# A quarter of one weight pair loaded in other row groups, and other runs of unused matmuls near the end

## The chip, the cores and the metric

The kernel runs on one core of one Trainium2 chip. A core has a matmul engine (TensorE, PE in the profile, with its weight loads as PEld), three engines for elementwise work (VectorE or DVE, ScalarE or ACT, GpSimd or POOL) and SyncE (SP), which here only starts output transfers. Transfers between main memory and the on-chip memory are carried out by 16 DMA engines that all queues share; a transfer counts as landed when the parts of all 16 have arrived. The metric is the time of one execution on the device in microseconds (us). Lower is better.

## The reference

The first half is attention for 8 batches, 8 heads, 576 positions and head size 64. Half of the heads look back over 32 neighbouring positions, the other half over 32 positions that are 4 apart. The second half takes the attention output as 4608 tokens of 512 numbers and runs a soft mixture of 8 experts with 4 slots each:

```
attn = softmax(mask(q @ k.T / 8)) @ v            # per batch and head
x = attn as [4608, 512]
logits = x @ phi                                  # phi [512, 32]
d = softmax over the tokens; slot_input = d.T @ x # 32 slots of 512
for e in range(8):                                # w1 [8,512,1024], w2 [8,1024,512]
    slot_out[e] = relu(slot_input[e] @ w1[e]) @ w2[e]
out = softmax over the slots(logits) @ slot_out   # [4608, 512]
```

The weights w1 and w2 hold 16.8 MB each in float32. They are used only once the slots of all tokens are summed, and each of their numbers is used for four slots alone.

## The kernel before, in words

**Attention.** The work is cut into 8 units: a pair of batches times a kind of head. For each unit GpSimd starts six loads of q, k and v (L425), which turn float32 into bfloat16 on the way into one of three slots of the buffer `stg`. TensorE transposes the unit (L566 or L571) into the buffer `TT`, multiplies q with k (L609), ScalarE takes the exponential (L616), VectorE masks it (L624), TensorE multiplies with v (L663), VectorE divides (L674), and so on up to the logits (L718) and the slot sums (L766). All these tiles go through the 8 banks of the accumulator memory, two at a time.

**Who decides the order.** Operations are listed in Python with a cost, a key and their dependences, and a planner (`Prog.schedule`) simulates the engines and fixes one order per engine. Dependences become waits on semaphores, one for each engine and one for each load. Loads are all issued by GpSimd in the order of the list, outputs all by SyncE. Where the planner sees TensorE idle inside a fixed window, it places runs of matmuls whose result nobody reads (L987).

**Weights.** `wload` fetches the weights under the attention and beyond it. The w1 parts go to `WD` and to a free stretch of `stg`. The w2 experts come in pairs: p3a (a part of the fourth pair) and p0, p1, p2 (the first three pairs), p3b and p3c (the rest of the fourth pair). They lie in places that attention no longer needs: p3a, p0 and p1 in `stg` (L469 for most, L458 to L463 for p0), p2, p3b and p3c in `TT`. One engine takes its share of these loads strictly in the order in which GpSimd issues them: w17, p3a, p0, p1, p2, p3b, p3c.

**The pair p0 is loaded in a special way.** Each of 128 partitions (rows) gets two runs of 4096 numbers. Rows 0 to 95 come as two ordinary loads (L458), one for each run. The last 32 rows, a quarter, come as four loads of 8 rows (L463), with one tiny load of 8 rows of 2 x 32 numbers into an unused buffer `scr` (L461) between the third and the fourth. All seven share one semaphore, `s_p0`.

**After attention.** A short chain on TensorE, VectorE and ScalarE computes the first expert layer (L838), folds it (L858) and copies it to `hT` (L867). Then the second layer runs part by part (L885) as the parts of w2 have landed, in the order p3a, p0, p1, p2, p3b, p3c. Between them stand the sums for the softmax over slots (`rsum`, L912) and one run of 7 unused matmuls (`keep`, L901), which is placed after p2. The sum of all parts is scaled into `so_sb` by VectorE and ScalarE (L923 and L927), and the last stage multiplies it with the token weights (L955, L957). VectorE and ScalarE take turns in scaling the results into float32 (L970, L969), and SyncE sends them out in six transfers of growing size (L978), 9.44 MB in all.

Of the kernel before, what the change touches and what calls it, by code (L numbers as in the profile page):

```python
# [52 lines left out]
class Op:  # L53
    n = 0
# [75 lines left out]
class Prog:  # L130
# [7 lines left out]
    def op(self, e, fn, r=(), w=(), a=(), alloc=(), cost=0.5, key=0.0, mode="f",  # L138
           sem=None, nbytes=0, nd=0, nq=1, ni=2, after=()):
        o = Op(e, fn, cost, key, mode)  # L140
        deps = list(after)
        for b in r:
            deps += b.ready
        for b in w:
            b.fresh()
            deps += b.prev
        for b in a:
            deps += b.prev
        seen = set()
        for d in deps:  # L150
            if d.id not in seen:
                seen.add(d.id)
                o.deps.append(d)
        for b in r:
            b.reads.append(o)
        for b in list(w) + list(a):
            b.ready.append(o)
        o.wr = [b for b in list(w) + list(a) if b.pool is not None]
        for b in list(r) + list(w) + list(a):
            if b.pool is not None and b not in o.touch:  # L160
                b.left += 1
                o.touch.append(b)
        o.alloc = list(alloc)
        o.sems = sem
        o.ni = ni + 2
        o.dma = nbytes / 435e3 + 0.011 * nd / 16 + 0.022 * nq
        self.ops.append(o)
        return o
# [149 lines left out]
def bass_dilated_sliding_attn__then__soft_moe_slots_kernel(  # L318
# [12 lines left out]
    op = P.op  # L331

    def sb(name, shape, dt=BF16):
        return A(nc.sbuf_tensor(name, shape, dt))

    WARM = 7
    NPT, NVN, NXB, NXT, NET = 6, 5, 5, 4, 2
    WD = sb("WD", [128, 7, 4096])
    stg = sb("stg", [128, 3, 9216])
# [22 lines left out]
    h_sb = sb("h_sb", [128, FF])  # L362
    hT = sb("hT", [128, 16, 128])
    half = sb("half", [128, 2, 32])
    scr = sb("scr", [8, 2, 32])
    so_sb = sb("so_sb", [128, DM])

    ps = A(nc.psum_tensor("ps", [128, 8, 512], F32))
# [11 lines left out]
    def tile(pool, size=1):  # L380
        t = Buf(pool)
        t.size = size
        return t
# [4 lines left out]
    def pair(t):  # L388
        return ps[:, t.phys[0]:t.phys[0] + 2, :]

    def bank(t):
        return ps[:, t.phys[0], :]
# [10 lines left out]
    b_mask = [Buf(), Buf()]  # L403
    b_id0, b_id, b_sel, b_fold, b_rowm, b_phist, b_phi = [Buf() for _ in range(7)]
# [36 lines left out]
    def wload(name):  # L441
        ap, b = HOME[name]
        b.prev = [o for al in b.al for o in al.ready + al.reads]
        sem = DmaSem(nc, f"s_{name}")
        if name[:2] == "w1":
            src = moe_w1[int(name[2:])].rearrange("(p c) f -> p c f", c=4)
            dst = ap.rearrange("p (c f) -> p c f", c=4)
        else:
            g = int(name[1])
            c = {"": slice(0, 16), "a": slice(0, 8), "b": slice(8, 14), "c": slice(14, 16)}[name[2:]]  # L450
            src = moe_w2[2 * g:2 * g + 2].rearrange("e (p c) f -> (e p) c f", c=16)[:, c, :]
            dst = ap.rearrange("p (c f) -> p c f", f=512)
        if name == "p0":
            src = src.rearrange("p (x c) f -> p x (c f)", x=2)
            dst = ap.rearrange("p (x y) -> p x y", x=2)[:, :, 0:4096]

            def skewed(g):
                res = [g.dma_start(dst[0:96, x], src[0:96, x]) for x in range(2)]  # L458
                for r in (96, 99, 97, None, 98):
                    if r is None:  # L460
                        res.append(g.dma_start(scr[:], src[0:8, :, 0:32]))  # L461
                    else:
                        res.append(g.dma_start(dst[r:128:4], src[r:128:4]))  # L463
                return res
            op("pool", skewed, after=b.prev, a=[b], cost=4.2, sem=sem, nbytes=512 * 8192, nd=288,
               nq=7)
            return
        cut = [slice(None)]
        op("pool", lambda g: [g.dma_start(dst[:, x], src[:, x]) for x in cut], after=b.prev, a=[b],  # L469
           cost=0.6 * len(cut), sem=sem, nbytes=512 * ap.shape[1], nd=128 * len(cut), nq=len(cut))  # L470

    for e in range(7):
# [12 lines left out]
       w=[b_phist], cost=0.1, sem=s_phi, nbytes=65536)  # L485
# [5 lines left out]
       r=[b_id0], w=[b_id], cost=1.6)  # L491
# [4 lines left out]
    def asel(t, sl, base, pat, cm):  # L496
# [7 lines left out]
       r=[b_mask[0]], w=[b_mask[1]], cost=0.6)  # L504
# [11 lines left out]
    for i, t in enumerate(VNt):  # L516
# [6 lines left out]
       cost=0.1, key=1)  # L523
    op("dve", lambda g: g.memset(half[:], 0.0), w=[b_half], cost=0.1, key=1)
    for x in range(2):
        for j in range(4):
# [3 lines left out]
               r=[b_id], w=[b_half], cost=0.1, key=1)  # L530
    for j in range(4):
        op("dve", lambda g, j=j: g.tensor_copy(fold[32 * j:32 * j + 32, :],
                                               ident[32 * j:32 * j + 32, 32 * j:32 * j + 32]),
           r=[b_id], w=[b_fold], cost=0.1, key=1)
    for j in range(4):
        op("dve", lambda g, j=j: g.tensor_copy(phi_pad[:, :, j, :], phi_st[:]),
           r=[b_phist], **{"w" if j == 0 else "a": [b_phi]}, cost=0.2, key=1)
# [244 lines left out]
    for u in range(NU):  # L782
# [28 lines left out]
    K1 = 1000.0  # L811
    op("dve", lambda vv: vv.tensor_reduce(rcs[:], csum[:], mybir.AxisListType.X, AluOp.add),
       r=[b_csum], w=[b_rcs], cost=0.1, key=K1)
# [3 lines left out]
    def pe_f(t):  # L817
# [9 lines left out]
        r=[fo], w=[b_siT], cost=0.25, key=K1)  # L827
# [5 lines left out]
    for hh in range(2):  # L833
        def pe(t, hh=hh):
            for c in range(4):
                for hi in range(2):
                    for j in range(4):
                        i_ = t.matmul(pair(hp)[32 * j:32 * j + 32, hh, :], siT[:, 512 * hi + 128 * c + 32 * j:  # L838
                                                       512 * hi + 128 * c + 32 * j + 32],
                                      w1v[2 * j + hi][:, c, 512 * hh:512 * hh + 512],  # L840
                                      start=(c == 0 and hi == 0), stop=(c == 3 and hi == 1))
            return i_
        ffn1 = op("pe", pe, r=[b_siT] + w1b, a=[hp], w=[b_hp[hh]], alloc=[hp] if hh == 0 else [],
                  cost=1.8, mode="c", key=K1, ni=64)
        if hh == 0:
            op("act", lambda ac: ac.activation(h_sb[:, 0:512], pair(hp)[:, 0, :], ACTF.Relu),
               r=[b_hp[0], hp], w=[b_h[0]], cost=0.65, key=K1)
        else:
            op("dve", lambda vv: vv.tensor_scalar(h_sb[:, 512:1024], pair(hp)[:, 1, :], 0.0, None,
                                                  op0=AluOp.max),  # L850
               r=[b_hp[1], hp], w=[b_h[1]], cost=0.65, key=K1)
    for p_ in range(2):
        ht = tile(psum, 1)

        def pe(t, p_=p_, ht=ht):
            for c in range(8):
                for x in range(2):
# [4 lines left out]
                 key=K1, ni=32)  # L862
# [16 lines left out]
    for k_, (name, g, c0, c1) in enumerate(PARTS):  # L879
        wv = HOME[name][0].rearrange("p (c f) -> p c f", f=512)  # L880
        for h_ in range(2):
            def pe(t, k_=k_, name=name, g=g, c0=c0, c1=c1, h_=h_, wv=wv):
                for c in range(c0, c1):
                    j = c % 4
                    i_ = t.matmul(pair(sp_)[32 * j:32 * j + 32, h_, 0:256],  # L885
                                  hT[:, c, 24 * g:24 * g + 32],
                                  wv[:, c - c0 + (1 if name == "p0" and c > 7 else 0), 256 * h_:256 * h_ + 256],
                                  start=(k_ == 0 and c < c0 + 4), stop=(k_ > 3 and c >= 12))
                return i_
            last_ = op("pe", pe, r=b_hT + [HOME[name][1]], alloc=[sp_] if k_ == h_ == 0 else [],  # L890
                       a=[sp_, b_sp[h_]], cost=0.13 * (c1 - c0) / 4, mode="c",
                       ni=2 * (c1 - c0),
                       key=K1 + 2 + 0.5 * k_ + 0.1 * h_)
            if k_ == 2:
                mid = last_
        if k_ == 3:
            warm = tile(psum, 1)

            def keep(t, warm=warm):
                for _ in range(WARM):  # L900
                    i_ = t.matmul(bank(warm)[:, 0:512], ident[:, :],  # L901
                                  mask[0][:].rearrange("p m x -> p (m x)")[:, 0:512],
                                  start=True, stop=True)
                return i_
            op("pe", keep, r=[b_id, b_mask[0]], w=[warm], alloc=[warm], cost=0.216 * WARM,
               ni=2 * WARM, key=K1 + 3.9, after=[last_])
    rs = tile(psum, 1)

    def rsum(t):
# [6 lines left out]
       after=[mid])  # L916
    op("dve", lambda vv: vv.reciprocal(rtok[:], bank(rs)[:, 0:N_TOK // 128]), r=[rs], w=[b_rtok],
       cost=0.2, key=K1 + 1)

    for h_ in range(2):  # L920
        sl = slice(256 * h_, 256 * h_ + 256)
        if h_ == 0:
            op("dve", lambda vv, sl=sl: vv.tensor_scalar(so_sb[:, sl], pair(sp_)[:, 0, 0:256],  # L923
                                                         rcs[:, 0:1], None, op0=AluOp.mult),
               r=[b_sp[0], b_rcs], w=[b_so[0]], cost=0.35, key=K1 + 20)
        else:
            op("act", lambda ac, sl=sl: ac.activation(so_sb[:, sl], pair(sp_)[:, 1, 0:256],  # L927
                                                      ACTF.Copy, scale=rcs[:, 0:1]),
               r=[b_sp[1], b_rcs], w=[b_so[1]], cost=0.4, key=K1 + 20)
# [12 lines left out]
    for o, (t0, n) in enumerate(TILES):  # L942
# [4 lines left out]
        for j0 in range(0, n, 2):  # L947
# [4 lines left out]
            for j in range(2 if split else min(2, n - j0)):  # L952
                def pe(t, o=o, po=po, j0=j0, j=j, split=split):
                    if split:
# [5 lines left out]
                        w=[b_po[j]], alloc=[po] if j == 0 else [], after=[p0] if j else [],  # L960
                        cost=0.12 if split else 0.22, key=kk + 0.01 * j)
                col = rcol[o] + (0 if split else j0 + j)

                def ev(en, po=po, ost=ost, j=j, j0=j0, split=split, col=col):
# [3 lines left out]
                    if en is nc.scalar:  # L968
# [3 lines left out]
                        cost=0.35 if split else 0.6, key=kk)  # L972
# [7 lines left out]
            r=[ob], cost=0.1, sem=so, nbytes=262144 * n, key=K1 + 30 + o)  # L980
# [60 lines left out]
```

## Time and profile before

Four runs of the kernel gave 180.01, 180.35, 180.52 and 181.2 us, with a median of 180.44 us.

| what | value |
|---|---|
| time of the profiled execution | 180.01 us |
| its span, first to last instruction | 178.3 us |
| mean granted TensorE clock | 0.911 |
| TensorE busy (matmul) | 136.0 us, 76% |
| VectorE busy | 112.9 us, 63% |
| ScalarE busy | 96.2 us, 54% |
| GpSimd busy | 37.7 us, 21% |
| read from main memory | 61.93 MB |
| written to main memory | 9.44 MB |
| loads issued by GpSimd (software queue) | 84.1% of the 16 DMA engines' span |

How to read it: "busy" is the time in which an engine ran an instruction. The "slices" view cuts the span into 40 equal parts and prints the busy share of each in tenths. PEclk is the clock that the chip grants TensorE, in tenths of full speed. The DMA line is the mean busy share of the 16 DMA engines. The "chain" follows the last instruction back to what released it, step by step. A "window" gives the same sums for one stretch of time; its last three columns are the granted clock, the DMA share and the rate in GB/s of bytes written. All times in the views are counted from the start of the span.

The trace also has a record for every packet that a DMA engine moved (start, duration, bytes) and for every arrival of an engine's part of a load. The records don't name the engine.

### The profile page before, as it was taken

How to read it: one execution, taken by the hardware profiler on the slowest of the kernel's cores; microseconds unless marked ns; L12 is line 12 of the kernel's file. 1: busy time of each engine (PE TensorE's matmuls, PEld its weight loads, DVE VectorE, ACT ScalarE, POOL GpSimd, SP SyncE). 2: the span in 40 equal slices, each digit the busy share in tenths (PEclk: the TensorE clock that was granted, in tenths of full speed). 3: DMA queues.
4: the chain of work that ended last, by engine and by line, in shares of the span. 5: the costliest groups of instructions: out<-in, count | busy, mean ns of one | idle time of the engine just before them, and what ended most of it. 6: DMA issues, size and time to landing. Idle time of an engine off the chain costs nothing.

```text
span 178.3 us, 5788 instructions
## 1 busy us (share of the span) xinstructions
PE 136.0 (76%) x2609; PEld 104.7 (59%) x2609; DVE 112.9 (63%) x256; ACT 96.2 (54%) x141; POOL 37.7 (21%) x75
## 2 busy tenths in 40 slices
PE   0019799777999877999967899978999997798000
PEld 0019687666797676798856788855556684342000
DVE  6850588766677992998979587998250200699300
ACT  2005889474695962878956688783211000599000
POOL 7990707034003300800103400102000000000000
PEclk9999999995699996999999699997899999699755
DMA  5999999999999999999999999999999996299995
GB/s 81 196 213 213 217 215 209 218 217 214 211 217 214 219 208 212 215 219 214 220 208 215 213 219 213 215 219 204 230 210 210 223 194 123 91 409 461 450 471 235
DMA packets 6056, 40.80 MB, mean 229 GB/s; under 512 B 1808, under 2 KB 1808, under 8 KB 2448
## 3 DMA queue, kind: packets, MB, share of 16 engines
q0 software_dynamic: 4640, 30.94, 84.1%
q1 hardware_dynamic: 1392, 9.50, 12.8%
q8 instruction: 20, 0.33, 0.7%
q14 instruction: 4, 0.03, 0.0%
HBM read 61.93 MB, written 9.44 MB: 400 GB/s over the span
## 4 chain that ended last, share of the span: by engine, by line
PE 38%; DMA 22%; DVE 19%; issue 6%; ACT 5%; POOL 2%; DVEq 0%; POOLq 0%
DMA TT<-in_moe_w_dram 17%; PE ps L571 8%; PE ps L566 6%; DMA stg<-in_k_dram 5%; PE ps L609 4%; DVE WD L970 4%; PE ps L663 4%; DVE PT L624 4%; PE ps L634 4%; PE ps L718 4%; DVE XB L674 4%; DVE VN L639 3%; PE ps L691 3%; ACT TT L591 2%; ACT PT L616 2%
## 5 line engine op out<-in xcount | busy, mean ns | idle before, releaser
L616 ACT ACTIVATE PT<-ps 128x768 bf16<-128x768 f32 x48 | 37.1, 811 | 10.4 <-PE ps L609 10.0
L591 ACT ACTIVATE TT<-ps 128x864 f32<-128x864 f32 x32 | 28.5, 896 | 18.6 <-PE ps L571 15.8
L674 DVE TENSOR_TENSOR XB<-ps,RV 96x768 bf16<-96x768 f32 x32 | 30.4, 951 | 0.9
L571 PE MATMUL ps<-ident,stg 96*64 96x96 bf16 x576 | 17.5, 225 | 13.9 <-DMA stg<-in_k_dram 12.8
L639 DVE COPY VN<-ps 128x768 bf16<-128x768 bf16 x32 | 17.1, 542 | 12.0 <-PE ps L634 11.9
L571 PEld LDWEIGHTS ps<-ident,stg 96*64 96x64 bf16 x576 | 15.6, 124 | 15.2 <-DMA stg<-in_k_dram 12.8
L663 PE MATMUL ps<-VN,PT 128*128 128x65 bf16 x384 | 18.5, 197 | 3.5 <-issue 2.2
L609 PE MATMUL ps<-TT 64*128 64x96 bf16 x384 | 16.8, 216 | 5.1 <-issue 3.2
L425 POOL DMA_DIRECT2D stg<-in_q_dram x16 | 8.8, 550 | 44.1 <-PE ps L571 23.8
L663 PEld LDWEIGHTS ps<-VN,PT 128*128 128x128 bf16 x384 | 15.2, 100 | 4.8 <-issue 2.3
L634 PE MATMUL ps<-ident,TT 128*128 128x128 bf16 x192 | 17.2, 234 | 0.5 <-ACT PT L616 0.4
L704 ACT ACTIVATE XT<-ps 128x576 bf16<-128x576 bf16 x22 | 13.7, 651 | 4.5 <-PE ps L691 4.5
L609 PEld LDWEIGHTS ps<-TT 64*128 64x128 bf16 x384 | 10.5, 100 | 9.1 <-issue 3.5
L691 PE MATMUL ps<-ident,XB 96*128 96x96 bf16 x192 | 13.4, 215 | 2.7 <-issue 1.6
L566 PE MATMUL ps<-ident,stg 96*128 96x96 bf16 x288 | 14.9, 206 | 0.2 <-DVE XB L674 0.2
L624 DVE TENSOR_TENSOR PT<-PT,mask_p 128x768 bf16<-128x768 bf16 x24 | 12.9, 551 | 2.7 <-ACT PT L616 2.2
L566 PEld LDWEIGHTS ps<-ident,stg 96*128 96x128 bf16 x288 | 13.2, 98 | 1.3 <-DVE XB L674 0.4
L634 PEld LDWEIGHTS ps<-ident,TT 128*128 128x128 bf16 x192 | 12.1, 104 | 2.7 <-ACT PT L616 0.5
L624 DVE TENSOR_TENSOR PT<-PT,mask_d 128x768 bf16<-128x768 bf16 x24 | 12.9, 545 | 1.1 <-ACT PT L616 1.1
L691 PEld LDWEIGHTS ps<-ident,XB 96*128 96x128 bf16 x192 | 10.3, 104 | 4.4 <-issue 2.3
L957 PE MATMUL ps<-so_sb,expT 128*128 128x512 bf16 x35 | 11.0, 448 | 0.2
L718 PE MATMUL ps<-XT,phi_pad 128*128 128x192 bf16 (+1 forms) x64 | 10.8, 319 | 0.2 <-ACT XT L704 0.2
(86 smaller groups left out, 175.7 us busy)
## 6 DMA issues: line engine op xcount, KB each, us to landing
WD<-in_moe_w_dram POOLq DMA_DIRECT2D x7, 1024.0 KB, 29.7
stg<-in_q_dram POOLq DMA_DIRECT2D x16, 288.0 KB, 19.0
stg<-in_v_dram POOLq DMA_DIRECT2D x16, 288.0 KB, 20.0
stg<-in_k_dram POOLq DMA_DIRECT2D x16, 288.0 KB, 20.9
out_dram<-WD SPq DMA_DIRECT2D x1, 4096.0 KB, 11.5
out_dram<-WD SPq DMA_DIRECT2D x1, 2304.0 KB, 7.1
stg<-in_moe_w_dram POOLq DMA_DIRECT2D x2, 1024.0 KB, 29.9
stg<-in_moe_w_dram POOLq DMA_DIRECT2D x1, 2048.0 KB, 25.8
```

The lines of the kernel that those rows point to most:

```text
L566: i_ = t.transpose(bankb2(pt, a)[:, 96 * kk:96 * kk + 96], two[:, j // 2, c, :], ident[0:96, 0:96])
L571: i_ = t.transpose(bankb2(pt, a)[64 * hx:64 * hx + 64, 96 * kk:96 * kk + 96], src[:, hx, c, :], ident[0:96, 0:96])
L591: return ac.activation(d, sv, ACTF.Copy)
L609: i_ = t.matmul(pair(sc)[:, hx, QB * x:QB * x + QB], win(u, 1, h01, blk_, bpar)[64 * hx:64 * hx + 64], win(u, 0, h01, blk_, bpar)[64 * hx: ...
L616: op("act", lambda ac: ac.activation(sbt(pt)[:, 0:768].rearrange("p (x n) -> p x n", x=2), pair(sc)[:, :, 0:384], ACTF.Exp, scale=SCALE), ...
L624: return dv.tensor_tensor(p_, p_, m.unsqueeze(1).to_broadcast([128, 2, 384]), AluOp.mult)
L634: i_ = t.transpose(bankb(pv)[:, 128 * m:128 * m + 128], win(u, 2, h01, m, bpar), ident[:, :])
L639: op("dve", lambda dv: dv.tensor_copy(sbt(vn)[:, :, :, 0:64], bankb(pv)[:, 0:768].rearrange("p (m x d) -> p m x d", m=6, x=2)), r=[pv], w= ...
L663: i_ = t.matmul(pair(po)[:, bk, 65 * po_:65 * po_ + 65], sbt(pts[i])[:, o_:o_ + 128], sbt(vn)[:, m, half, 0:65], start=True, stop=True)
L674: op("dve", lambda dv: dv.tensor_tensor(sbt(xb)[:].rearrange("p m (x h d) -> p h x m d", x=2, h=2)[:, h01], pv()[:, :, :, 0:64], sbt(rv)[: ...
L691: i_ = t.transpose(bankb(px)[:, QB * m:QB * m + QB], sbt(xb)[:, m, 128 * x:128 * x + 128], ident[0:QB, 0:QB])
L718: i_ = t.matmul(o_, phi_pad[:, c].rearrange("p j i -> p (j i)"), rhs, start=c == 0, stop=c == 3)
```

## The change

Two edits. The last 32 rows of p0 are cut in other groups, listed in `TURNS` as (number of rows, first row, step), with tiny loads where the first row is `None`:

- 2 rows (126 and 127), then a tiny load of 14 rows
- 7 rows (96, 99, ... 114), then 9 rows (117 to 125)
- 7 rows (97, 100, ... 115), then a tiny load of 9 rows
- 7 rows (98, 101, ... 116)

That makes nine loads for p0 in place of seven. The tiny loads go to separate parts of a larger `scr`.

The runs of unused matmuls become two: 4 of them with a place after p1 and 8, in place of 7, after p2. In the order that the planner makes, the run of 4 stands between `rsum` (L912) and the matmuls of p2. All other instructions keep their order and their waits on every engine.

```diff
-    WARM = 7
+    WARM = {2: 4, 3: 8}
+    TURNS = ((2, 126, 1), (14, None, 0), (7, 96, 3), (9, 117, 1), (7, 97, 3), (9, None, 0), (7, 98, 3))
...
-    scr = sb("scr", [8, 2, 32])
+    scr = sb("scr", [16, len(TURNS), 2, 32])
...
             def skewed(g):
                 res = [g.dma_start(dst[0:96, x], src[0:96, x]) for x in range(2)]
-                for r in (96, 99, 97, None, 98):
+                for i, (n, r, step) in enumerate(TURNS):
                     if r is None:
-                        res.append(g.dma_start(scr[:], src[0:8, :, 0:32]))
+                        res.append(g.dma_start(scr[0:n, i], src[0:n, :, 0:32]))
                     else:
-                        res.append(g.dma_start(dst[r:128:4], src[r:128:4]))
+                        e = r + step * (n - 1) + 1
+                        res.append(g.dma_start(dst[r:e:step], src[r:e:step]))
                 return res
-            op("pool", skewed, after=b.prev, a=[b], cost=4.2, sem=sem, nbytes=512 * 8192, nd=288,
-               nq=7)
+            op("pool", skewed, after=b.prev, a=[b], cost=0.6 * (2 + len(TURNS)), sem=sem, nbytes=512 * 8192,
+               nd=288, nq=2 + len(TURNS))
...
-        if k_ == 3:
+        if k_ in WARM:
             warm = tile(psum, 1)
 
-            def keep(t, warm=warm):
-                for _ in range(WARM):
+            def keep(t, warm=warm, n=WARM[k_]):
+                for _ in range(n):
                     i_ = t.matmul(bank(warm)[:, 0:512], ident[:, :],
                                   mask[0][:].rearrange("p m x -> p (m x)")[:, 0:512],
                                   start=True, stop=True)
                 return i_
-            op("pe", keep, r=[b_id, b_mask[0]], w=[warm], alloc=[warm], cost=0.216 * WARM,
-               ni=2 * WARM, key=K1 + 3.9, after=[last_])
+            op("pe", keep, r=[b_id, b_mask[0]], w=[warm], alloc=[warm], cost=0.216 * WARM[k_],
+               ni=2 * WARM[k_], key=K1 + (3.9 if k_ == 3 else 3.2), after=[last_])
```

## The prediction

> **What bounds the kernel now.** I read the chain of waits first. It leaves the attention at 119.75 us and runs through one transfer to 152 us:
>
> ```profile
> 120.03 1.07 POOL TT L469 x2
> 121.10 30.92 DMA TT<-in_moe_w_dram
> 152.01 0.04 issue
> 152.06 0.30 PE ps L885 x2
> 152.39 0.49 DVE so_sb L923
> ```
>
> The transfer is p3c, the last weight part. Its two matmul groups (L885) release `so_sb`, the last stage and the outputs. So 31 us are set by the end of the weight loads. TensorE's timeline says how much of that TensorE could have made good:
>
> ```profile
> 145.14 2.17 PE L912 MATMUL ps<-rowm,expT 128*128 128x1 bf16 x36
> 147.24 1.06 PE L885 MATMUL ps<-TT,hT 128*32 128x256 bf16 x32
> 148.23 1.69 PE L901 MATMUL ps<-mask_p,ident 128*128 128x512 bf16 x7
> 150.81 0.61 PE L885 MATMUL ps<-TT,hT 128*32 128x256 bf16 x12 [0.89 <-DMA TT<-in_moe_w_dram]
> 152.06 0.40 PE L885 MATMUL ps<-TT,hT 128*32 128x256 bf16 x4 [0.64 <-DMA TT<-in_moe_w_dram]
> ```
>
> TensorE waits only for p3b (0.89) and p3c (0.64); up to p2 it is the bound itself. Windows of half a microsecond show how the loads end (the last two columns are the DMA share and GB/s):
>
> ```profile
> 149.00:149.50 0.50, 0.50 (x4) 0.20 (x2) 0.00 (x0) 0.00 (x0) 0.00 (x0) 1.00 0.82 156
> 149.50:150.00 0.50, 0.41 (x2) 0.00 (x0) 0.00 (x0) 0.00 (x0) 0.00 (x0) 1.00 0.60 123
> 150.00:150.50 0.50, 0.00 (x0) 0.00 (x0) 0.00 (x0) 0.00 (x0) 0.00 (x0) 1.00 0.27 49
> 150.50:151.00 0.50, 0.19 (x8) 0.20 (x10) 0.00 (x0) 0.00 (x0) 0.00 (x0) 1.00 0.20 37
> 151.00:151.50 0.50, 0.42 (x12) 0.13 (x4) 0.00 (x0) 0.00 (x0) 0.00 (x0) 1.00 0.13 25
> ```
>
> From 150 us on only a few of the 16 DMA engines still work, and everybody waits for them. Which ones, the packet records tell. Packets of one engine follow each other 606 ns apart (8192 bytes written, 625 ns each with a little overlap), so they can be sorted into 16 chains. At the end of p3a, ahead of p0, seven engines are early (113.6 to 114.1), one is between (114.8), eight are late (115.9 to 116.5). The late ones have carried the instruction fetches, packets of 16384 bytes that take about 0.95 us; their durations repeat with period eight, so the fetches go round eight engines, two each by then. In p0's tail each load of 8 rows lands on eight engines, alternately one half (I call it A: three loads) and the other (B: one load and the tiny one). A holds five early engines, the one between and two late ones. The ends of p3c follow: B's two early ones 147.2 and 147.4, A's five early ones 149.3 to 149.5, B's six late ones 149.7 to 151.0 (those above 150 had one more fetch), the one between 150.5, A's two late ones 151.5 and 151.7. The arrival is recorded 0.36 later: 152.02. From p3a to p3c an engine needs 35.6 with three tail rows, 33.3 with one: 1.17 a row. A late fetch adds 1.0 to 1.5.
>
> Last, the clock, in windows of its own length of 3.41 us:
>
> ```profile
> 119.14:122.55 3.41, 1.92 (x48) 1.53 (x45) 3.38 (x9) 1.80 (x4) 1.61 (x3) 1.00 1.02 207
> 122.55:125.97 3.42, 3.42 (x21) 1.89 (x18) 1.80 (x3) 0.83 (x2) 0.00 (x0) 0.50 1.13 206
> ...
> 149.86:153.27 3.41, 1.40 (x20) 0.76 (x20) 0.50 (x2) 0.47 (x1) 0.00 (x0) 1.00 0.11 21
> 153.27:156.69 3.42, 3.42 (x10) 1.22 (x8) 3.11 (x5) 2.53 (x4) 0.00 (x0) 0.50 0.51 200
> ```
>
> After a window with TensorE busy 56% (1.92) or 41% (1.40) the next one runs at half clock. Windows at 70% and more weren't followed by that.
>
> **What the Trainium skill says.** "DMA: Bandwidth & Descriptors", section on why a DMA increments its semaphore by 16: a load issued by GpSimd whose slowest dimension is k below 16 goes to k consecutive engines from a round-robin cursor. The alternating halves A and B agree. The same page, latency and other measured facts, calls engines 7 and 15 usually slower than the rest; the trace shows one engine 0.8 behind seven, and eight behind for another reason, the fetches. "TensorE: Matmul & The Clock Gate", part 1: the clock is decided in free-running windows of about 3.4 us; the two pairs above agree. "SBUF — State Buffer", door 1: four neighbouring partitions share one DMA port. No row here shows four engines writing to one port; two do so in the q, k, v loads at 9216 bytes in 700 ns, the same rate.
>
> **The tail loads.** 2 + 14 = 16 and 7 + 9 = 16, so the cursor comes back to its start S after each pair. The two engines from S get 4 rows, the next five 3, the other nine 1. The sum is 8 + 15 + 9 = 32 rows, as before. It fits the pattern of seven early engines exactly if S is the first of them. Then: early with 4 rows 114.0 + 33.3 + 3 x 1.17 = 150.8; early with 3 rows 149.6; the one between 114.8 + 33.3 = 148.1; late with 1 row 149.2 to 149.8, and up to 151.0 with a fetch. The last arrival becomes 151.0 + 0.36 = 151.35, against 152.02: 0.7 earlier.
>
> Unknown is S. In this execution A starts two engines behind the first early one. The old loads move the cursor by 40, which is 8 beyond a full turn, the new ones by 55, which is 7 beyond. If it is kept between executions it wanders; if it is reset, S depends on how often the kernel ran before. Bounds: 0.9 earlier at best (150.8 + 0.36), and for the worst see the rivals.
>
> Ports: the load of rows 117 to 125 has four rows (120 to 123) on one port. At worst they take twice the time, 1.2 more on four late engines; at best nothing, since these engines reach the row at different times. I take nothing to 0.5 in the range. A tail load that an engine takes no row of costs it three marks of four bytes, some 0.036 us: a late engine sits out four instead of three, nothing to speak of. The larger tiny loads (packets of 26 ns) cost 0.05.
>
> **GpSimd.** Two more issues at about 0.56 each (L463 and L461) put p1 back by 1.1 in GpSimd's queue. Hidden: p1's issue waits 11.46 us for TensorE (L566) anyway, and the engines reach the tail at 121.1, 21 us after its last issue at 99.6. If that cover were gone, 1.1 would be added.
>
> **The unused matmuls.** L901 costs 1.69 / 7 = 0.24 each, 0.216 in a long run. Four before p2: 0.87. Eight instead of seven: 0.22. In the present order p2 starts at 147.24 with its load landed at 147.10, so it moves to 148.1, ends its issue at 149.1; eight more end at 150.85. p3b, which starts at 150.81 now, starts at 150.85: no loss, but also a floor. p3b needs about 0.40 of issue, so p3c can't start before 151.25. Of the 0.7 won by the loads, 0.7 can be used (152.06 to 151.35), no more than 0.8.
>
> They also close TensorE's gaps: the 0.89 before p3b is gone. In a window like 149.86 to 153.27 TensorE would be busy about 0.97 + 0.5 + 0.4 and, if p3c is 0.7 earlier, 1.1 of the last stage: 2.9 of 3.41, 85%. So the half clock after it should go. In the profile it makes the first seven L957 take 0.42 each instead of 0.22. What that costs is the underfilled start of the outputs: the DMA share from 154.4 to 157 lacks about 0.6 us, of which I take 0.3 as won (0 to 0.5), since VectorE and ScalarE at 0.69 each become the next bound. After that the outputs fill the DMA engines, and an earlier start passes through to the end one for one.
>
> **The sum.** 180.01 - 0.7 - 0.3 = 179.0 on the profiled execution. Its 180.01 is the fastest of four, 0.43 under the median; since the luck of clock window and fetch can matter less in the new form, I add half of that: 179.2.
>
> **The rivals.** *The loads don't shift what is last* (the change doesn't do what it says). If S is where this trace has it, the seven engines with 3 or 4 rows hold one late engine; it still ends at 151.5, and only the clock is won: 179.7 to 180.3. For it: this very trace. Against: the two kernels move the cursor by different amounts. *Ports.* The four rows on one port take the 0.7 back on late engines: 180.0. *Late engines are loaded more* (slower). If S lies six to fifteen engines beyond the first early one, a late engine with a fetch gets three rows or a late engine four: 116.5 + 33.3 + 3 x 1.17 = 153.3, up to 154.3 with a fetch, p3c lands 153.7 to 154.7, that is 1.7 to 2.7 later, TensorE falls idle and half clock stays: 181.6 to 182.7. It decides as soon as one late engine holds four rows, or three and a fetch in the tail. For it: nothing in the kernel sets the cursor, and ten of sixteen places do it. Against: the old kernel has the same weakness, and three of its four runs lie within 0.5 us.
>
> **How the numbers follow.** Loads shifted as laid out: 0.48, around 179.2, its own range 178.6 to 179.7. Nothing shifted 0.10, ports 0.07, both near 180.0. Late engines loaded more 0.35, around 181.9. A change of 0.5% is 0.9 us, about what a measurement of this kernel can tell from none. Faster (under 179.5) holds most of the first case, 0.42; slower (over 181.3) is the last case, 0.35; the rest, 0.23, is within. The range for 8 in 10 must reach into the slow case: 178.6 to 182.2.
>
> **What would show it.** Right: p3c lands near 151.3, the DMA share falls from 0.8 to nothing within a microsecond, TensorE has no wait over 0.2 before p3b, L957 runs at full clock. Wrong: p3c lands at 152 or later, with one or two engines alone at work after 151.

## The result and the profile after

The changed kernel takes 181.64 us in the median of 33 runs, the kernel before, on the same chip, 180.37 us in 54. The ratio is 1.0075 with a 95% interval of 1.0057 to 1.0092: slower, by 1.3 us. The profiled execution of the changed kernel took 181.29 us (span 179.5, mean granted clock 0.930), that of the kernel before 180.01 (178.3, 0.911). Times below are medians of all runs, while a ratio leaves out the few runs over 1.5% above their kernel's fastest, so it can differ from the quotient of the medians. The line numbers of the changed kernel are two higher in the second half (L885 is L887, L901 is L903, L957 is L959).

The chain of waits of the kernel after. Its columns are start, duration, and what it was:

```profile
121.36 1.07 POOL TT L471 x2
122.43 31.20 DMA TT<-in_moe_w_dram
153.63 0.04 issue
153.68 0.30 PE ps L887 x2
154.00 0.49 DVE so_sb L925
```

The same transfer ends the same chain, but p3c now lands at 153.63 where it landed at 152.02. The 1.6 us are more than the whole difference of the two executions (181.29 - 180.01 = 1.28). p3c is also issued 1.3 us later (121.36 against 120.03), but that is not what makes it land late: two experiments below issue it at 119.36 and 122.57 and have it land at 153.64 and 153.29. So the loss lies in the loads ahead of it. TensorE's timeline of the kernel after (start, busy time, instructions, and in brackets the wait ahead of them):

```profile
148.38 1.02 PE L903 MATMUL ps<-mask_p,ident 128*128 128x512 bf16 x4
149.33 1.06 PE L887 MATMUL ps<-TT,hT 128*32 128x256 bf16 x32
150.32 1.90 PE L903 MATMUL ps<-mask_p,ident 128*128 128x512 bf16 x8
152.70 0.61 PE L887 MATMUL ps<-TT,hT 128*32 128x256 bf16 x12 [0.48 <-DMA TT<-in_moe_w_dram]
153.68 0.40 PE L887 MATMUL ps<-TT,hT 128*32 128x256 bf16 x4 [0.36 <-DMA TT<-in_moe_w_dram]
154.78 2.42 PE L959 MATMUL ps<-so_sb,expT 128*128 128x512 bf16 x10
```

Both runs of unused matmuls are where they should be, and TensorE still comes early for p3b (0.48 of waiting) and p3c (0.36). It is itself 2.1 us later at p2 than before (149.33 against 147.24): 1.3 of that it had already when the second layer began (144.18 against 142.84), the rest is the run of 4. Since p3b's load is waited for after that, none of it sets the end. How the loads end, in windows of half a microsecond of the kernel after (the last three columns are the granted clock, the DMA share and GB/s):

```profile
151.00:151.50 0.50, 0.50 (x4) 0.26 (x3) 0.00 (x0) 0.00 (x0) 0.00 (x0) 1.00 0.48 90
151.50:152.00 0.50, 0.50 (x4) 0.11 (x2) 0.00 (x0) 0.00 (x0) 0.00 (x0) 1.00 0.11 16
152.00:152.50 0.50, 0.22 (x2) 0.00 (x0) 0.00 (x0) 0.00 (x0) 0.00 (x0) 1.00 0.14 25
152.50:153.00 0.50, 0.30 (x10) 0.29 (x12) 0.00 (x0) 0.00 (x0) 0.00 (x0) 1.00 0.15 29
153.00:153.50 0.50, 0.32 (x8) 0.03 (x2) 0.00 (x0) 0.00 (x0) 0.00 (x0) 1.00 0.05 8
```

Two things are to be seen. At 151.0 to 151.5 the DMA share is 0.48 where the kernel before had 0.13: seven engines are still at work then, not two. And from 151.5 to 153.3 a share of 0.11 to 0.15 is two engines of sixteen, alone at work. Sorted into sixteen chains as in the prediction, the packets give the ends of p3c by engine: the nine with one row (three early, six late) 147.6 to 150.6, the early ones with three or four rows and the one between 151.3 to 151.8, and two late ones with three rows 153.20 and 153.28. Both of these had an instruction fetch in the tail (144.8 and 150.5), about 0.9 us each; the last two of the kernel before kept their pace from p1 on, without one. So part of the 1.6 us is the luck of this one execution. The mean over all sixteen says less by luck: it is 150.61, in the kernel before 149.77, so an engine lost 0.84 us on average with the same weights to carry.

Where it was lost shows in one window, 121 to 127 us, in which the engines do p0's last quarter. First the kernel before, then the kernel after:

```profile
121.00:127.00 6.00, 5.28 (x50) 3.37 (x50) 3.95 (x7) 2.10 (x5) 0.64 (x2) 0.72 1.12 213
```

```profile
121.00:127.00 6.00, 4.56 (x51) 3.03 (x48) 4.65 (x10) 2.10 (x4) 1.61 (x3) 0.73 1.13 182
```

The DMA share is the same, 1.12 and 1.13, so the engines are no less busy, but the rate fell from 213 to 182 GB/s. Six microseconds at 31 GB/s less are 186 kB, which take 0.87 us at 213, close to the mean loss of 0.84.

The packet records show the same thing directly. In both kernels most packets of 8192 bytes take 625 ns and most of 16384 bytes 1227 ns. In p0's last quarter some take longer: up to 948 ns for 8192 bytes in the kernel before, up to 1246 in the kernel after. All that the packets of these two sizes took beyond their usual time between 112 and 152 us, shared among sixteen engines, is 0.39 us in the kernel before and 1.20 in the kernel after. The difference, 0.81, is nearly the whole mean loss. The bytes are the same; it is their packets that became slower.

The clock at the outputs became full, as predicted. In the slices of the kernel after, the granted clock is full over the whole end of the second layer and the outputs (slices 31 to 37 of 40; before, slice 35 stood at 6), and in the groups view the last stage's matmuls fell to 395 ns from 448:

```profile
PEclk9999999996999997999999699997899999999755
...
L959 PE MATMUL ps<-so_sb,expT 128*128 128x512 bf16 x35 | 10.1, 395 | 0.4 <-DVE WD L972 0.2
```

That the two runs of unused matmuls brought this is not shown: every experiment below that keeps the old run of 7 has full clock there too, and in the kernel after the window ahead of the outputs (151.08 to 154.50) had TensorE busy for 63%, not for the 85% that the prediction counted on.

### The profile page after: what moved, and what is told of

Read it like the earlier page. It is cut to its first block, busy times and chain, and to the rows that moved or that the text cites. A ratio compares the mean times of both kernels' runs of the same rounds, so it can differ in the third digit from the quotient of the medians.

```text
span 179.5 us, 5800 instructions
## 1 busy us (share of the span) xinstructions
PE 135.7 (76%) x2614; PEld 104.5 (58%) x2614; DVE 112.6 (63%) x256; ACT 96.4 (54%) x141; POOL 38.8 (22%) x77
## 4 chain that ended last, share of the span: by engine, by line
PE 42%; DMA 22%; DVE 15%; issue 6%; ACT 5%; POOL 2%; DVEq 0%; POOLq 0%
DMA TT<-in_moe_w_dram 17%; PE ps L573 9%; PE ps L665 6%; PE ps L568 6%; PE ps L611 5%; PE ps L636 5%; DVE WD L972 5%; DMA stg<-in_k_dram 5%; PE ps L693 4%; PE ps L720 4%; DVE PT L626 2%; DVE XB L676 2%; ACT PT L618 2%; ACT TT L593 2%; DVE VN L641 2%
## 5 line engine op out<-in xcount | busy, mean ns | idle before, releaser
L959 PE MATMUL ps<-so_sb,expT 128*128 128x512 bf16 x35 | 10.1, 395 | 0.4 <-DVE WD L972 0.2
L720 PE MATMUL ps<-XT,phi_pad 128*128 128x192 bf16 (+1 forms) x64 | 10.1, 306 | 0.2 <-ACT XT L706 0.2
```

The lines of the kernel that those rows point to most:

```text
L720: i_ = t.matmul(o_, phi_pad[:, c].rearrange("p j i -> p (j i)"), rhs, start=c == 0, stop=c == 3)
```

## The experiments

All kernels keep the computation; two say below what they change in it. Each ratio is to runs of the kernel before on the same chip, with its 95% interval. The edits are shown against the changed kernel, in which `TURNS` lists (rows, first row, step) and `WARM` the unused matmuls after a part.

### Which of the two edits

Loads of before, unused matmuls of after:

```diff
-    TURNS = ((2, 126, 1), (14, None, 0), (7, 96, 3), (9, 117, 1), (7, 97, 3), (9, None, 0), (7, 98, 3))
+    TURNS = ((8, 96, 4), (8, 99, 4), (8, 97, 4), (8, None, 0), (8, 98, 4))
```

> The loads of before with the two runs of unused matmuls of after (4 and 8). Theory (the loads are what made it slower, by rows on shared ports and by late engines that hold three rows): no slower than before, 0 to 0.5 us faster, ratio 0.997 to 1.000, with full clock in the window after 153 us. Rival (the longer runs stand on TensorE's path): slower by up to the 1.1 us of the five added matmuls, ratio 1.004 to 1.006.

Measured: 180.27 us, ratio 1.0003 (0.9978 to 1.0028). The unused matmuls neither cost nor bring anything that shows. In its profiled execution they did stand on the chain that ended last: p2 came late (147.63), the eight unused matmuls after it ran mostly at half clock (2.61 us), and TensorE, not p3c, set the end.

Loads of after, unused matmuls of before:

```diff
-    WARM = {2: 4, 3: 8}
+    WARM = {3: 7}
```

> The loads of after with the one run of 7 unused matmuls of before. Theory (loads): all of the loss, 1.0 to 1.6 us, ratio 1.006 to 1.009, and half clock returns for the first matmuls of the last stage. Rival (runs): as fast as before, ratio 0.998 to 1.002.

Measured: 181.16 us, ratio 1.0057 (1.0030 to 1.0084). The loads carry the loss. In the chain of waits of this kernel p3c lands at 153.16, and the window of p0's last quarter has the same low rate as that of the kernel after:

```profile
121.50 31.66 DMA TT<-in_moe_w_dram
153.20 0.31 PE ps L887 x2
```

```profile
121.00:127.00 6.00, 4.92 (x57) 3.79 (x55) 4.11 (x8) 1.74 (x3) 1.05 (x2) 0.72 1.14 178
```

One part of the expectation was missed: half clock did not return for the first matmuls of the last stage.

```profile
L959 PE MATMUL ps<-so_sb,expT 128*128 128x512 bf16 x34 | 9.9, 394 | 0.6 <-issue 0.2
```

It fell on 149.44 to 152.85 instead, after a window in which TensorE was busy for 75%. In the kernel before, windows of 70% and more were not followed by half clock, and in the kernel after one of 63% was not. So the busy share of a window does not foretell the clock of the next as simply as the prediction took it.

### The rows' neighbourhood or their split over the engines

Two things differ in the new loads: which engines take how many rows, and how close together the rows of one load lie on the partitions. Before, the 8 rows of a load are four partitions apart; after, 7 rows are three apart, and the 9 and the 2 are neighbours.

First only the neighbourhood: the counts of before, so each engine takes as many rows as it did before, but 8 neighbouring rows in each load.

```diff
-    TURNS = ((2, 126, 1), ... (7, 98, 3))
-    WARM = {2: 4, 3: 8}
+    TURNS = ((8, 96, 1), (8, 104, 1), (8, 112, 1), (8, None, 0), (8, 120, 1))
+    WARM = {3: 7}
```

> Before, with the same four loads of 8 rows and the same tiny load, but each load takes 8 neighbouring rows instead of every fourth one: the same engines with the same counts, only other partitions, four neighbours on one port. Theory of ports: the tail of p0 takes longer on all engines, 0.8 to 1.5 us slower, ratio 1.004 to 1.008. Theory of the cursor alone (only which engine holds how many rows counts): no change, ratio 0.998 to 1.002.

Measured: 181.39 us, ratio 1.0063 (1.0035 to 1.0091), p3c at 153.64 in its profile. Only the places of the rows differ from the kernel before, and a loss as large as that of the changed loads (1.0057) is there. The rate in the same window of this kernel:

```profile
121.00:127.00 6.00, 5.51 (x52) 3.80 (x54) 3.71 (x8) 2.47 (x5) 0.00 (x0) 0.72 1.11 172
```

A row lies somewhere in main memory and somewhere on the partitions, and both became neighbours. The next two take these apart. In both the last quarter of p0 lands in another order of rows, so the output is not the reference's; the amount of work is the same. `j` counts the four loads of 8 rows; counts and unused matmuls are those of before.

```diff
                         e = r + step * (n - 1) + 1
-                        res.append(g.dma_start(dst[r:e:step], src[r:e:step]))
+                        j = (0, 1, 2, None, 3)[i]
+                        near, far = slice(96 + 8 * j, 104 + 8 * j), slice(96 + j, 128, 4)
+                        res.append(g.dma_start(dst[near], src[far]))      # e5; in e6: dst[far], src[near]
```

> Before, but each of the four loads of 8 rows writes 8 neighbouring partitions while it still reads every fourth row of the weights (p0's last quarter lands in another order, so the output is not the reference's; the work is the same). Theory of shared ports on the writing side: slower like the kernel with adjacent rows on both sides, ratio 1.004 to 1.008. Rival (neighbouring addresses in main memory): ratio 0.998 to 1.002.

> The reverse: reads 8 neighbouring rows of the weights and writes every fourth partition (again p0's last quarter in another order). Theory of ports on the writing side: ratio 0.998 to 1.002. Rival (main memory): ratio 1.004 to 1.008.

Measured: neighbours on the partitions 181.57 us, ratio 1.0077 (1.0053 to 1.0102); neighbours in main memory 180.42 us, 1.0022 (0.9995 to 1.0048), which can't be told from none. It is the side that is written to that carries the loss. (The one profile of the first is of its longest run, 182.72 us, so nothing is read from it.) The Trainium skill says in "SBUF — State Buffer", door 1, that four neighbouring partitions share one DMA port, and by its table rows 96 to 127 lie on eight of the sixteen ports. Rows four apart then meet eight ports, eight neighbours meet two. The runs agree with this: neighbours are slower. The records show longer packets, but not what happens at a port, so the shared port as the reason is argued from the page's map and not shown.

The opposite experiment keeps what the change did to the split, and puts the rows four apart again, all but the two of the first load. To fit, the 9 rows become 8 and 1, which is one load more and the same engines.

```diff
-    TURNS = ((2, 126, 1), (14, None, 0), (7, 96, 3), (9, 117, 1), (7, 97, 3), (9, None, 0), (7, 98, 3))
-    WARM = {2: 4, 3: 8}
+    TURNS = ((2, 125, 1), (14, None, 0), (7, 96, 4), (8, 99, 4), (1, 124, 1), (7, 97, 4), (9, None, 0), (7, 98, 4))
+    WARM = {3: 7}
```

> Every engine takes part in exactly the tail rows that it takes part in after the change (two engines of the later group keep three rows, two of the earlier group get four), but the rows of one load are four partitions apart as before the change, and the run of 7 unused matmuls is that of before. If the loss comes from rows of one load that lie close together on the partitions: as before, ratio 0.999 to 1.003, last weights at 151.9 to 152.5. If it comes from the two later engines with three rows and an instruction fetch: as the changed loads alone, ratio 1.004 to 1.008, last weights at 153.0 or later. Both at work: between them.

Measured: 179.48 us, ratio 0.998 (0.9952 to 1.0008). This interval and that of the same split with rows close together (1.0030 to 1.0084) don't meet, though the two were run on different chips, each against the kernel before there. 12 of its 21 runs are below 180 us, and none of the 15 with rows close together. Its rate is that of the kernel before:

```profile
121.00:127.00 6.00, 4.99 (x49) 3.51 (x50) 4.06 (x7) 2.05 (x5) 0.71 (x2) 0.72 1.10 216
```

So the loss comes from the rows' neighbourhood, and the split, for which the loads were recut, is worth 0.2% in the middle of its interval, which includes no gain at all. The expectation was half missed: the ratio lies just below the 0.999 to 1.003 of the first case, and in its profiled execution (180.75 us, one of its longer ones) p3c landed at 153.14 and not by 152.5. One engine ended at 152.79, all others by 151.18.

An earlier try at another split had most rows four apart and three neighbours: four rows on engines 0 to 2, three on 3 to 6, one on 7 to 14, none on 15, counted from where the turn begins.

```diff
+    TURNS = ((3, 124, 1), (13, None, 0), (7, 96, 4), (9, None, 0), (7, 97, 4), (9, None, 0), (7, 98, 4), (8, 99, 4))
```

> After, with the same kind of split (seven engines with 3 or 4 rows, nine with one or none) but each load of 7 and 8 rows takes every fourth row, so that only a load of 3 rows has neighbours (loads of 3, 7, 7, 7 and 8 rows, tiny ones of 13, 9 and 9). Theory of ports: 0.5 to 1.5 us faster than after, that is ratio to before 0.996 to 1.003. Theory of the cursor alone: as slow as after, ratio 1.006 to 1.009, since a late engine still holds three rows in most executions.

Measured: 181.0 us, ratio 1.0015 (0.9989 to 1.0042), rate 206 GB/s, its last two engines at 152.3 and 152.5. (Without its four longest runs, as in the ratio, the median is 180.82.) It can't be told from no change, and it lies between the kernel before and the changed loads in rate and ratio alike.

### Where the turn over the engines begins

The prediction left open where the first tail load begins on the sixteen engines. If the loads of before are shifted by tiny loads ahead of them (and a rest behind, so that the sum is four whole turns), the eight engines with three rows change.

```diff
+    TURNS = ((14, None, 0), (8, 96, 4), (8, 99, 4), (8, 97, 4), (8, None, 0), (8, 98, 4), (10, None, 0))   # e7
+    TURNS = ((6, None, 0), (8, 96, 4), (8, 99, 4), (8, 97, 4), (8, None, 0), (8, 98, 4), (2, None, 0))     # e8
+    WARM = {3: 7}
```

> Before with a tiny load of 14 rows ahead of the four loads and one of 10 rows behind them: the cursor is moved by 64 in all, four whole turns, and the eight engines with three rows are two places further back than in the profile of before. Theory (the cursor is carried from execution to execution, and which engines hold three rows sets the end): the place is the same in every execution, either the early engines and the one between (p3c near 151.3, 0.5 to 1.0 us faster, ratio 0.994 to 0.998) or all late ones (p3c at 153.5 or later, 1.0 to 2.0 us slower), and the spread of the times is smaller than before's. Rival (the cursor does not matter): ratio 0.998 to 1.002 and the same spread.

> As the last one, with tiny loads of 6 and 2 rows: 48 in all, three whole turns, and the eight engines with three rows lie six places further on. Theory: the other one of the two cases, that is slow where the last one is fast and fast where it is slow; the two differ by 1.5 to 2.5 us. Rival: both as before.

Measured: back 181.34 us, ratio 1.0076 (1.0045 to 1.0106); on 180.9 us, 1.0059 (1.0030 to 1.0087). The two were to lie apart by 1.5 to 2.5 us, on either side of the kernel before. They lie 0.4 apart, both slower, which is not what early engines that lie next to each other would give. The chains of waits, of the shift back first:

```profile
120.67 33.31 DMA TT<-in_moe_w_dram
154.03 0.30 PE ps L887 x2
```

```profile
120.85 32.40 DMA TT<-in_moe_w_dram
153.28 0.31 PE ps L887 x2
```

Counted from the engine where the turn begins, and taking that to be the same one in each profiled execution, the chains of before, after and these two fit one map: early are engines 0, 1, 2, 7, 15, one of 3 to 5 and one of 8 to 13; one of 3 to 5 is between; the other eight, 6 and 14 among them, are late. In this map the early engines that the prediction needed next to each other are not. The shift on gives three rows mostly to late engines, at an unhurt rate of 211 GB/s, and that would be why it is slower. The shift back has two late engines with three rows, as before, and rows four apart, yet a rate of 191 GB/s, longer packets (1.10 us per engine, counted as above) and a mean end of 150.34; why isn't settled.

A tiny load of 8 rows at the end makes the rows issued for p0's quarter 48, three whole turns:

```diff
+    TURNS = ((8, 96, 4), (8, 99, 4), (8, 97, 4), (8, None, 0), (8, 98, 4), (8, None, 0))
+    WARM = {3: 7}
```

> The kernel before with one more tiny load of 8 rows at the end of the five, so that the rows issued in all are a whole number of turns over the sixteen engines (48 in place of 40). If the turn were carried over from one execution to the next, the times of before, which alternate between about 179.5 and 180.7 from one execution to the next, would come from it: then no alternation here, and a ratio of 0.995 or 1.004. If every execution begins its turn at the same engine and the alternation comes from where the instruction fetches fall: the alternation stays, ratio 0.999 to 1.002, and the profile shows the last weights at 151.9 to 152.5.

Measured: 180.12 us, ratio 1.0007 (0.9981 to 1.0034). The times of before fall into two levels: of 73 runs in this batch, 27 lie between 179.02 and 179.82, 46 from 180.01 to 181.59. The padded kernel has both levels too (10 of 21 below 180), though no longer in regular alternation. So a turn carried from one execution to the next isn't what makes them. In its profile p3c landed at 153.29, not by 152.5: one of the two last engines still had an instruction fetch of 0.89 us at 151.2.

### Other splits

No skew at all: p0 as two ordinary loads of 128 rows, eight rows to an engine.

```diff
-                res = [g.dma_start(dst[0:96, x], src[0:96, x]) for x in range(2)]
+                res = [g.dma_start(dst[:, x], src[:, x]) for x in range(2)]
-    TURNS = ((2, 126, 1), ... (7, 98, 3))
-    WARM = {2: 4, 3: 8}
+    TURNS = ()
+    WARM = {3: 7}
```

> Without any skew: the first quarter of the pair comes in two loads of all 128 rows, as the others do, eight rows to an engine. An engine of the later group then has two rows to do in the tail where before it has one (1.17 us more): 149.7 to 150.97 becomes 150.9 to 152.1, and the last weights land at 151.5 to 152.5. If the split by engine is what counts: ratio 0.997 to 1.003. If few loads with rows far apart cost less at the ports too: 0.994 to 0.998.

Measured: 179.37 us, ratio 0.9967 (0.9945 to 0.9988). It beats both kernels: the one before by 0.33%, and the changed one, whose interval against before begins at 1.0057. 18 of its 21 runs are on the lower level, against 27 of 73 of the kernel before in the same batch. In its profiled execution (179.64 us) the rate of the window is whole, and its timeline shows a short wait for p3c:

```profile
121.00:127.00 6.00, 5.12 (x63) 3.33 (x65) 4.23 (x9) 2.47 (x5) 0.53 (x1) 1.00 1.03 217
```

```profile
151.00 0.65 PE L887 MATMUL ps<-TT,hT 128*32 128x256 bf16 x12
152.03 0.40 PE L887 MATMUL ps<-TT,hT 128*32 128x256 bf16 x4 [0.38 <-DMA TT<-in_moe_w_dram]
```

The late engines, with two rows each, end between 150.0 and 151.7, the last one with a fetch at 148.9. In the kernel after, where late engines with three rows were hit, the last ones ended at 153.2 and 153.3.

The rows given out by the map above: engines 0, 1, 2 four, 7 and 15 three, 3 to 5 two, the rest one, in eleven loads.

```diff
+    TURNS = ((16, 96, 2), (6, 97, 6), (1, None, 0), (1, 123, 1), (7, None, 0), (4, 99, 6), (4, None, 0), (1, 125, 1), (7, None, 0), (4, 101, 6), (13, None, 0))
+    WARM = {3: 7}
```

> The 32 rows of the last quarter given out by what the traces show of each engine: 0, 1, 2 four rows, 7 and 15 three, 3, 4, 5 two (two of these three early or between, one late), the other eight one; rows of one load two or six partitions apart; 11 loads in place of 5. If the engines begin where the profiles show it and a row costs 1.17 us: no late engine has three rows, the last ends between 150.9 and 151.6, last weights at 151.3 to 151.9, ratio 0.996 to 0.999. If more loads cost as much as they save, or the ports set the end: 1.000 to 1.005.

Measured: 180.87 us, ratio 1.0042 (1.0016 to 1.0068), rate 185 GB/s, mean end of p3c 150.78. The rate is as low as that of the changed loads, and p3c landed at 153.07, not by 151.9 as expected. The first load has 16 rows two apart, which by the page's table puts two rows on each port; that this is the cause was not tried by itself.

All together, in the order of the rate between 121 and 127 us. The third column is the time that the packets took beyond their usual time, in us per engine, counted as in the section on the result. Rate and packets are of one execution each.

| loads | GB/s | longer packets | ratio to before |
|---|---|---|---|
| 8 neighbours per load | 172 | 1.34 | 1.0063 |
| changed loads alone | 178 | 1.44 | 1.0057 |
| changed kernel | 182 | 1.20 | 1.0075 |
| by engine, 16 rows two apart | 185 | 1.14 | 1.0042 |
| shift back | 191 | 1.10 | 1.0076 |
| neighbours in main memory only | 205 | 0.22 | 1.0022 |
| another split, mostly four apart | 206 | 0.54 | 1.0015 |
| shift on (late engines loaded) | 211 | 0.10 | 1.0059 |
| before | 213 | 0.39 | 1 |
| changed split, four apart | 216 | 0.16 | 0.9980 |
| before, padded | 216 | 0.30 | 1.0007 |
| before, changed unused matmuls | 216 | 0.23 | 1.0003 |
| no skew | 217 | 0.04 | 0.9967 |

With one exception, the shift on, which loads six late engines with three rows, slower packets and a slow kernel go together.

## Why the prediction was wrong

It took faster, 179.2 us, as likeliest; the kernel is slower. The measured 181.64 lies inside its range of 178.6 to 182.2, near the upper end. That part of the range was meant for late engines loaded with more rows, which is not what made the kernel slow, so that it lies inside is luck.

- **The bound: right.** p3c's arrival sets the end before and after, and it is the end of the loads that moved. Of the 1.6 us between its two arrivals a part is the fetches of one execution.
- **Tail loads, 0.7 won: wrong.** The step that failed is "It fits the pattern of seven early engines exactly if S is the first of them". By the map above, which takes the turn to begin at the same engine each time, there is no such S: the early engines don't lie next to each other. The new split leaves two late engines with three rows, as the old one did, and they end last, at 153.2 in the profile after. This is the rival that "the loads don't shift what is last", held at 0.10; with the rows set four apart the split measures 0.998.
- **Ports, "nothing to 0.5": wrong, and the term that decided.** It was looked for where four rows meet on one port, and put on four late engines that reach them at different times. In the profiles the sixteen engines lost 0.84 us on average, and by the page's map rows three apart also meet: the rate fell by 31 GB/s for six microseconds, packets took up to twice their time, and the ratio went from 1.0057 to 0.998 when the rows were set four apart. That the packets of the q, k and v loads kept their rate was no guide to this. The rival "Ports" had the place, and 180.0 for its time, because it set the cost against a gain that wasn't there.
- **Late engines loaded more (0.35, 181.6 to 182.7): the right time, by another cause.** Its picture, a late engine with three rows and a fetch, is in the profile after. But the same split with rows four apart has the same engines and is not slower. What it adds over the kernel before isn't shown.
- **Unused matmuls at no cost: right**, 1.0003. The run of 4 took 1.02 (0.87 predicted), the run of 8 1.90 (1.91 predicted).
- **The clock: right by luck.** The half clock at the outputs is gone, but the window that was to be 85% busy was 63%, and the kernels with the old run of 7 unused matmuls have full clock there as well. So the step from busier TensorE to full clock is not borne out. Its gain of 0.3 us doesn't show in the runs of that edit alone, whose interval of some 0.45 us to either side doesn't exclude it either.
- **GpSimd's further issues hidden: right.** The split with one load more than the change (ten for p0) is not slower than before.
- **The sum.** With nothing won by the split, -0.3 not seen, and the slower packets at +0.9 in place of nothing, the profiled execution would have been put at 180.9, against 181.29. Between the changed loads with rows close together and the same split with rows apart the ratios say 1.4 us (0.77%); the half microsecond over the mean loss of some 0.85 isn't settled.

## What to carry to other kernels

When part of a load is handed out row by row, the rows in flight together must also lie apart on the partitions they are written to: here neighbours cost 0.6 to 0.8% of the kernel, and four apart cost nothing that shows, but for one shifted order (1.0076) whose slow packets are not explained. A DMA share that stays while GB/s falls is how it looks in a window of the profile, and packets that take longer than others of their size show it directly. And before skewing a load to favour engines that seem early, measure the plain load: here it beat both skews.

## What the runs showed that was not expected

- Eight of the engines are about 2.2 us late at p3a (115.9 to 116.5 against 113.6 to 114.1), which agrees with the instruction fetches: their durations repeat with period eight, and two each by then, of about 0.95 us, are an estimated 1.9 us. In the map above these eight don't all lie next to each other. The Trainium skill, "DMA: Bandwidth & Descriptors", latency and other measured facts, calls engines 7 and 15 usually slower; no run here shows whether they are, since the records don't name the engines and the numbers of this map are counted from where the turn begins.
- One tail fetch of 0.89 us on an engine that is last anyway moves p3c: 153.20 and 153.28 in the kernel after were both so hit. With the plain load 18 of 21 runs stay below 180 us, with the skewed one 27 of 73. What decides which executions of a kernel are on the upper level was not followed in the trace.
- No kernel went below 178.95 us, whatever its loads; the lowest time of six experiments lies between 179.01 and 179.13. What holds them there was not tested: no run removed TensorE work.
